# Expert slots that hold a row's id and gate instead of the row, with the rows fetched from the output

## Chip, cores, metric

The kernel runs on one core of one Trainium2 chip. The metric is the device time of that core in microseconds, median of several runs. An engine is one of the core's five instruction streams: TensorE (PE, its weight loads PEld), VectorE (DVE), ScalarE (ACT), GpSimd (POOL) and SyncE (SP), which here issues nearly all DMAs.

## What is computed

First a linear attention with a state for each of 4 batches x 8 heads, 768 steps, 48 channels, then a mixture of 8 experts over the 3,072 rows of 384 numbers (8 heads x 48) that come out of it:

```python
for t in range(S):                                   # B, H, S, D = 4, 8, 768, 48
    state = alpha[:, :, t, :, None] * state + np.einsum('bhd,bhe->bhde', k[:, :, t], v[:, :, t])
    y[:, :, t] = np.einsum('bhd,bhde->bhe', q[:, :, t], state)
x = y.transpose(0, 2, 1, 3).reshape(B * S, H * D)    # 3072 x 384
out = x.copy()
xc = x[x @ w_skip > 0]                               # only these rows see an expert
e_idx = np.argmax(xc @ w_gate, axis=1)               # one of E = 8
gate_w = softmax(xc @ w_gate)[chosen expert]
h = np.maximum(xc[e_idx == e] @ w1[e], 0.0)          # 384 -> F = 1024
out[those rows] = xc + gate_w * (h @ w2[e])          # 1024 -> 384
```

So about half of the rows are left as they are, and each of the others goes through one expert.

## The kernel before

**Attention.** `static_path` runs 24 chunks: chunk i holds the heads of batch i % 4 for 128 steps. The rows of a chunk come out as one tile `x` of 128 rows x 386 numbers: 384 of the row, one for its id (its number in the output) and one for its gate. In chunk order, VectorE does two scans over the decays (`decay`, L233 and L241, written three chunks ahead of their use), GpSimd multiplies them into k and q (L244, L245), TensorE makes the scores (L254), the transposes of k (L268), the products with the state (`inter`), with v (`outer`, `intra`) and the turn back to rows together with the router's products (`rows`, L337); VectorE updates the state (`carry`, L322 and L325). ScalarE copies the rows to `x` (L343), and SyncE stores them in the output (L345): every row is written there, and the rows that pass an expert are written again later. The instructions of an engine run in the order in which the program is written (`manual_schedule`); a tile pool with n buffers makes a writer wait for the readers of n tiles before.

The inputs of a chunk are loaded by SyncE four chunks ahead (`load`, L217 for the first five, L220 and L223): `qka` (decays, q and k; five buffers, two DMAs of 48x1541 for a chunk) and `vt` (128x384). On the same queue go the row stores, the pieces of the experts' weights (`weight_pieces`, L492, 128x768 of `raw`, which has two buffers) and the clears, below.

**Routing.** `route_expert` (groups of three chunks) and `route_one` (the last six chunks singly) find the expert of each row, its gate and whether it is skipped; `route_rank` and `route_slot` make from running counts a slot number: row n of expert e goes to slot e*3072 + n, a skipped row to a number out of bounds, which the DMA drops. `scatter` (L474, GpSimd) writes the 128 rows of `x`, 386 numbers each, into their slots of `xs` in DRAM. An expert has 256 slots that are used (a run with more is done again by a general path, which does not run here). The slots that no row takes must hold something: `clear_pieces` (L141 to L150) writes zeros and an id out of bounds into 256 slots of each expert, eight DMAs of 386 KB, two in each of the first four chunks, from a tile `empty` that GpSimd fills (L146, L147).

**The seam.** The experts use rows of all chunks, but expert 0 starts before the last three chunks (21 to 23, `LATE` = 21 and above) have been scattered: `early_rows` (L435) loads expert 0's 256 slots as they are, with the rows of chunks 0 to 20, and `early_turn` (L449) transposes them on TensorE; the rows of the last three chunks are added by products with a matrix of ones and zeros (`late_rows`, from high and low parts made by `late_split`, L456 and L457, into the same sums). The last three scatters stand behind that in the program.

**Experts.** For each expert `gather` (L530) loads its 256 slots with two DMAs of 128 rows into `xr` (three buffers), two experts ahead; `turn` (L557) transposes them on TensorE, ScalarE and VectorE split them in high and low parts; `up` (L577) makes 18 products of 128x128 by 128x256 for a pair of column blocks, ScalarE (L581) and VectorE (L582) take the relu and split it, `down` (L593) makes 24 products for each half, VectorE (L596) multiplies by the gate `xr[:, j, 385]` and adds the row, and GpSimd scatters 128 rows to the output by their ids (L598). Both products run three times, high by high, low by high and high by low. The weights are split in the same way by ScalarE (`hi`, L508) and by VectorE or GpSimd (`lo`, L512; tiles `w1h`, `w1l`, `w2h`, `w2l`) for the next expert while one runs. During the first experts `guard` loads all alphas (L541, `alpha`, one buffer) and ScalarE looks whether one lies outside a range (L545, `over`).

## Time and profile before

| | |
|---|---|
| time, median of 3 runs | 333.29 us (332.33 to 333.87) |
| profiled execution: its time | 333.48 us |
| its span | 331.8 us |
| mean granted clock of TensorE | 0.917 |
| TensorE busy (products / weight loads) | 292.5 / 270.2 us, 88% / 81% |
| VectorE, ScalarE, GpSimd busy | 226.9, 152.6, 184.3 us (68%, 46%, 56%) |
| DMA | 66.15 MB in 29,420 packets, mean 199 GB/s; 4,466 packets under 512 B |

How to read it: the span goes from the first to the last instruction that the profiler shows; the time of the run is 1.7 us more. The page gives the span in 40 slices with the busy share of each engine in tenths. A row of an engine in order of time reads: start, duration (both us), engine, line, operation, output <- inputs, shapes, how many, and in brackets the idle time of that engine ahead of it with what ended it. SPq is the part of SyncE that issues DMAs; its durations are those of the issuing, not of the transfer. A busy share is a mean over stages in which different engines set the pace, so the stages are looked at one by one.

### The profile page before, as it was taken

How to read it: one execution, taken by the hardware profiler on the slowest of the kernel's cores; microseconds unless marked ns; L12 is line 12 of the kernel's file. 1: busy time of each engine (PE TensorE's matmuls, PEld its weight loads, DVE VectorE, ACT ScalarE, POOL GpSimd, SP SyncE). 2: the span in 40 equal slices, each digit the busy share in tenths (PEclk: the TensorE clock that was granted, in tenths of full speed). 3: DMA queues.
4: the chain of work that ended last, by engine and by line, in shares of the span. 5: the costliest groups of instructions: out<-in, count | busy, mean ns of one | idle time of the engine just before them, and what ended most of it. 6: DMA issues, size and time to landing. Idle time of an engine off the chain costs nothing. (4 is left out here: it accounts for less than half of the span.)

```text
span 331.8 us, 7365 instructions
## 1 busy us (share of the span) xinstructions
PE 292.5 (88%) x2778; PEld 270.2 (81%) x2778; DVE 226.9 (68%) x453; ACT 152.6 (46%) x298; POOL 184.3 (56%) x205
## 2 busy tenths in 40 slices
PE   5877879998699986858898999999999999999991
PEld 5766768887588775646677999999999899999991
DVE  8995578899979999999437664738183555455320
ACT  5122422353435414402424657958595976455200
POOL 6093432589888988866524445444655355464311
PEclk9578785999879999995959999999999999999997
DMA  7949999999976867773546574949688586751000
GB/s 230 281 133 250 252 283 250 223 257 224 236 148 152 183 157 176 197 193 97 155 125 201 166 235 157 398 137 379 215 285 314 193 331 229 242 172 63 12 19 29
DMA packets 29420, 66.15 MB, mean 199 GB/s; under 512 B 4466, under 2 KB 15456, under 8 KB 29376
## 3 DMA queue, kind: packets, MB, share of 16 engines
q1 hardware_dynamic: 26816, 60.76, 63.6%
q0 software_dynamic: 2560, 4.83, 4.2%
q8 instruction: 24, 0.39, 0.5%
q14 instruction: 20, 0.16, 0.2%
HBM read 52.87 MB, written 15.77 MB: 207 GB/s over the span
## 5 line engine op out<-in xcount | busy, mean ns | idle before, releaser
L254 PE MATMUL ps_s<-qka 48*128 48x128 f32 x384 | 31.8, 308 | 23.8 <-POOL qka L244 12.0
L244 POOL TENSOR_TENSOR qka<-qka,sfx 112x512 f32<-112x512 f32 x22 | 27.7, 1257 | 42.4 <-DVE sfx L241 30.7
L254 PEld LDWEIGHTS ps_s<-qka 48*128 48x128 f32 x384 | 26.9, 209 | 29.0 <-POOL qka L244 13.5
L582 DVE SCALAR_TENSOR_TENSOR hl<-ps_h,hh 128x512 fp32r<-128x512 f32 x32 | 22.1, 690 | 33.5 <-ACT hh L581 33.3
L593 PE MATMUL ps_o<-w2h,hh 128*128 128x384 f32 x128 | 43.6, 341 | 0.0
L598 POOL DMA_INDIRECT out_dram<-o,xr x16 | 18.6, 1162 | 45.0 <-DVE o L596 45.0
L593 PE MATMUL ps_o<-w2h,hl 128*128 128x384 f32 x128 | 43.0, 336 | 0.0
L593 PE MATMUL ps_o<-w2l,hh 128*128 128x384 f32 x128 | 43.0, 336 | 0.0
L233 DVE TENSOR_TENSOR_SCAN pfx<-qka,seed 112x516 f32<-112x516 f32 x24 | 34.0, 1418 | 11.0 <-DMA qka<-in_qka_dram 11.0
L343 ACT COPY x<-ps_g 128x384 f32<-128x384 f32 x23 | 11.0, 480 | 65.5 <-DVE logit L338 23.7
L512 POOL TENSOR_TENSOR w2l<-raw,w2h 128x512 fp32r<-128x512 f32 x24 | 31.2, 1302 | 13.5 <-ACT w2h L508 13.1
L474 POOL DMA_INDIRECT xs<-x,slot x24 | 29.9, 1244 | 12.2 <-DVE on L386 4.9
L577 PE MATMUL ps_h<-xh,w1h 128*128 128x256 f32 x192 | 34.2, 284 | 1.2 <-DVE hl L582 1.2
L310 ACT COPY xt<-ps_y 48x512 f32<-48x512 f32 x48 | 27.8, 580 | 13.6 <-PE ps_y L305 12.8
L577 PE MATMUL ps_h<-xh,w1l 128*128 128x256 f32 x192 | 33.8, 282 | 0.0
L241 DVE TENSOR_TENSOR_SCAN sfx<-qka,seedb 112x515 f32<-112x515 f32 x24 | 32.3, 1347 | 1.5
L577 PE MATMUL ps_h<-xl,w1h 128*128 128x256 f32 x192 | 33.3, 282 | 0.0
L305 PE MATMUL ps_y<-st,vt 128*48 128x128 f32 x384 | 32.9, 313 | 0.0
L512 POOL TENSOR_TENSOR w1l<-raw,w1h 128x512 fp32r<-128x512 f32 x16 | 22.3, 1395 | 18.7 <-issue 10.4
L581 ACT ACTIVATE hh<-ps_h 128x512 fp32r<-128x512 f32 x32 | 19.1, 597 | 27.6 <-PE ps_h L577 27.6
L261 DVE COPY_PREDICATED st<-mask,ps_s 128x1024 f32<-128x1024 uint8 x24 | 30.9, 1286 | 0.0
L596 DVE SCALAR_TENSOR_TENSOR o<-ps_o,xr 128x384 f32<-128x384 f32 x16 | 9.9, 616 | 30.3 <-PE ps_o L593 30.3
(141 smaller groups left out, 667.5 us busy)
## 6 DMA issues: line engine op xcount, KB each, us to landing
raw<-in_w_dram SPq DMA_DIRECT2D x64, 384.0 KB
qka<-in_qka_dram SPq DMA_DIRECT2D x38, 288.9 KB
vt<-in_v_dram SPq DMA_DIRECT2D x24, 192.0 KB
out_dram<-x SPq DMA_DIRECT2D x24, 192.0 KB
alpha<-in_nat_dram SPq DMA_DIRECT2D x8, 576.0 KB
xr<-xs SPq DMA_DIRECT2D x18, 193.0 KB
xs<-empty SPq DMA_DIRECT2D x8, 386.0 KB
qka<-in_first_dram SPq DMA_DIRECT2D x3, 674.2 KB
```

What stands on the lines that cost most here:

```text
L233: nc.vector.tensor_tensor_scan(pfx[:PD].rearrange("p a t -> p (a t)"), w["qka"][:PD, 0:n], self.seed1[:PD], 0.0, ALU.mult, ALU.max)
L241: nc.vector.tensor_tensor_scan(sfx[:PD, 0:n - 1][:, ::-1], w["qka"][:PD, 2:AW][:, ::-1], seed[:PD, 2:AW][:, ::-1], 0.0, ALU.mult, ALU.add)
L244: (eng or nc.gpsimd).tensor_tensor(w["kh"][:PD], w["kh"][:PD], after, ALU.mult)
L254: nc.tensor.matmul(ps[:, h, p * P:(p + 1) * P], lhsT=kh[r, p, :], rhs=qh[r, p, :], start=True, stop=True)
L261: self.nc.vector.copy_predicated(w["st"], self.mask, w["ps"])
L305: nc.tensor.matmul(ps[h][64 * h:64 * h + D, p, :], lhsT=v[:, o:o + D], rhs=w["st"][:, h, p * P:(p + 1) * P], start=(i < B and p == 0), sto ...
L310: nc.scalar.copy(out=xt[r], in_=ps[h][r])
L474: ins = nc.gpsimd.indirect_dma_start(out=self.xs[:, :], out_offset=bass.IndirectOffsetOnAxis(ap=self.slot[:, i, :], axis=0), in_=x, in_off ...
L512: eng.tensor_tensor(lo[:, s], raw[:, s], hi[:, s].bitcast(F32), ALU.subtract)
L577: nc.tensor.matmul(ps[:, u, :], lhsT=a[:, k, f * P:(f + 1) * P], rhs=b[:, k, :], start=(n == 0), stop=(n == len(order) - 1))
L582: nc.vector.scalar_tensor_tensor(out=hl, in0=ps, scalar=0.0, in1=hh.bitcast(F32), op0=ALU.max, op1=ALU.subtract)
L593: nc.tensor.matmul(ps, lhsT=a[:, f, js], rhs=b[:, f, :], start=(n == 0), stop=(n == 3 * FT - 1))
```

## The change

A slot of `xs` is now 8 bytes, id and gate; the rows themselves are read back from the output, where `rows` has stored them.

- `empty` is a constant of 128x2x2 numbers, filled at the start by VectorE and GpSimd. One clear of 16 KB for all experts stands in chunk 2 of the loop (L152 in the new numbering), instead of eight in chunks 0 to 3.
- The slots are laid out so that partition p holds slots 2p and 2p+1 (`slots`, and `slots0_i` to match).
- `scatter` (L497) writes 8 bytes a row.
- `early_rows` loads the ids and gates of expert 0 (`meta`, SyncE) and then fetches its rows from the output with two indirect DMAs of GpSimd (`fetch_rows`, L457) into `xr0`. A slot without a row keeps what its buffer held, so `xr0` is zeroed at the start by two ScalarE copies. From this tile `clear_late` also writes zeros into the output rows of chunks 21 to 23 (three DMAs of 192 KB, in chunk 14), which get their own values later. The stores of the rows of chunks 22 and 23 wait for the two early fetches, which read the output.
- `metas` loads the ids and gates of all experts with one DMA behind the last scatter (1,024 pieces of 16 B). `gather` fetches the rows of an expert with two indirect DMAs of GpSimd into one of three buffers that VectorE zeroes once (`xrb`). Those of experts 1 and 0 are issued behind the first quarter of expert 0's `up`; those of expert e + 2 behind `turn(e + 1)` instead of at the start of expert e.
- The gate and the id in `down` come from `meta`, and `xr` has 384 columns.

```diff
-        self.xs = dram.tile([E * N, XW], F32, name="xs")
+        self.xs = dram.tile([E * N, 2], F32, name="xs")
...
-    def clear_pieces(self):
-        nc = self.nc
-        empty = self.const.tile([P, XW], F32, name="empty")
-        nc.gpsimd.memset(empty, 0.0)
-        nc.gpsimd.iota(empty[:, DM:DM + 1].bitcast(I32), pattern=[[0, 1]], base=OFF, channel_multiplier=0)
-        for e in range(E):
-            yield nc.sync.dma_start(out=self.xs[e * N:e * N + CAP, :].rearrange("(j p) w -> p j w", p=P),
-                                    in_=empty.unsqueeze(1).to_broadcast([P, NB, XW]))
+    def slots(self, e0, e1):
+        return self.xs.rearrange("(e n) w -> e n w", e=E)[e0:e1, :CAP, :].rearrange("e (p j) w -> p e (j w)", j=NB)
+
+    def clear(self):
+        nc = self.nc
+        nc.sync.dma_start(out=self.slots(0, E),
+                          in_=self.empty.rearrange("p j w -> p (j w)").unsqueeze(1).to_broadcast([P, E, 2 * NB]))
+
+    def clear_late(self):
+        nc = self.nc
+        for i in range(LATE, NT):
+            row = self.row(i)
+            nc.sync.dma_start(out=self.out[row:row + P, :], in_=self.xr0[:, 0, :])
...
     def early_rows(self):
-        for j in range(NB):
-            ins = nc.sync.dma_start(out=self.xr0[:, j, :], in_=self.xs[j * P:(j + 1) * P, :])
-            self.after(ins.ins, "xs")
-            self.early.append(ins.ins.name)
+        meta = self.late.tile([P, NB, 2], F32, name="meta0")
+        ins = nc.sync.dma_start(out=meta.rearrange("p j w -> p (j w)"), in_=self.slots(0, 1).rearrange("p e w -> p (e w)"))
+        self.after(ins.ins, "xs")
+        self.early = [ins.ins.name]
+        self.fetch_rows(self.xr0, meta)
+
+    def fetch_rows(self, xr, meta):
+        return [self.nc.gpsimd.indirect_dma_start(
+            out=xr[:, j, :], out_offset=None, in_=self.out[:, :],
+            in_offset=bass.IndirectOffsetOnAxis(ap=meta[:, j, 0:1].bitcast(U32), axis=0),
+            bounds_check=N - 1, oob_is_err=False) for j in range(NB)]
...
-            in_=x, in_offset=None, bounds_check=E * N - 1, oob_is_err=False)
+            in_=x[:, DM:DM + 2], in_offset=None, bounds_check=E * N - 1, oob_is_err=False)
...
+        self.xrb = [self.mp.tile([P, NB, DM], F32, name=f"xr{i}", bufs=1) for i in range(3)]
+        for t in self.xrb:
+            self.nc.vector.memset(t, 0.0)
+
+    def metas(self):
+        self.meta = self.mp.tile([P, E, NB, 2], F32, name="meta", bufs=1)
+        ins = self.nc.sync.dma_start(out=self.meta.rearrange("p e j w -> p e (j w)"), in_=self.slots(0, E))
+        self.after(ins.ins, "xs")
 
     def gather(self, e):
-        xr = self.mp.tile([P, NB, XW], F32, name="xr", bufs=3)
-        for j in range(NB):
-            s = e * N + j * P
-            ins = self.nc.sync.dma_start(out=xr[:, j, :], in_=self.xs[s:s + P, :])
-            self.after(ins.ins, "xs")
-        self.ew[e] = dict(xr=xr)
+        xr, meta = self.xrb[e % len(self.xrb)], self.meta[:, e]
+        for ins in self.fetch_rows(xr, meta):
+            self.disjoint(ins.ins, "out")
+        self.ew.setdefault(e, {}).update(xr=xr, meta=meta)
...
                 if i + 4 < NT:
                     self.load(i + 4)
-                advance(clear, 2)
+                if i == 2:
+                    self.clear()
+                if i == 14:
+                    self.clear_late()
...
-            for e in (1, 0):
-                self.gather(e)
+            self.metas()
...
-                if e + 2 < E:
-                    self.gather(e + 2)
                 for g in range(FT // 2):
                     self.up(e, g)
                     advance(split, 2)
+                    if (e, g) == (0, 0):
+                        for n in (1, 0):
+                            self.gather(n)
                 if e + 1 < E:
                     self.turn(e + 1)
+                if e + 2 < E:
+                    self.gather(e + 2)
```

How the order of two engines changes, at the two places of which the prediction speaks. SyncE's queue from the load of chunk 4's `vt` on (`qka` with its buffer's number, `xs<-empty` the clears, `out_dram<-x` the store of a chunk's rows, `raw` a piece of weights), before:

```order
L223 DMA vt<-in_v_dram 128x384
L149 DMA xs<-empty 128x2x386 x2
L220 DMA qka_128<-in_qka_dram 48x1541 x2
L223 DMA vt<-in_v_dram 128x384
L149 DMA xs<-empty 128x2x386 x2
L345 DMA out_dram<-x 128x384
L220 DMA qka_129<-in_qka_dram 48x1541 x2
L223 DMA vt<-in_v_dram 128x384
```

and after:

```order
L240 DMA vt<-in_v_dram 128x384
L237 DMA qka_132<-in_qka_dram 48x1541 x2
L240 DMA vt<-in_v_dram 128x384
L362 DMA out_dram<-x 128x384
L237 DMA qka_133<-in_qka_dram 48x1541 x2
L240 DMA vt<-in_v_dram 128x384
L152 DMA xs<-empty 128x8x4
```

The two pairs of clears that stood ahead of the loads of chunks 5 and 6 are gone, and the one that is left stands behind them; the store of chunk 0's rows keeps its place ahead of the load of chunk 6.

GpSimd where the experts begin (`w1l`, `w2l`: low parts of expert 1's weights; `xr_...<-out_dram` a fetch of 128 rows, of expert 1, of expert 0 and of expert 2 in this order; `out_dram<-o` the scatter of an expert's result), before:

```order
L474 DMA xs<-x,slot 24576x386 x3
L512 TENSOR_TENSOR w1l<-raw,w1h 128x512 x2
L512 TENSOR_TENSOR w2l<-raw,w2h 128x512
L598 DMA out_dram<-o,xr 3072x384
L512 TENSOR_TENSOR w2l<-raw,w2h 128x512
```

and after:

```order
L497 DMA xs<-x,slot 24576x2 x3
L535 TENSOR_TENSOR w1l<-raw,w1h 128x512
L457 DMA xr_2328<-out_dram,meta 128x384 x2
L457 DMA xr_2327<-out_dram,meta 128x384 x2
L535 TENSOR_TENSOR w1l<-raw,w1h 128x512
L535 TENSOR_TENSOR w2l<-raw,w2h 128x512
L457 DMA xr_2329<-out_dram,meta 128x384 x2
L628 DMA out_dram<-o,meta 3072x384
```

Four fetches have come between the two `w1l` pieces, and two more ahead of the first scatter to the output; before, rows came by SyncE's plain loads and none of this stood on GpSimd.

26 lines of the change are left out of this document (16 added, 10 removed).

## Prediction

> **What bounds the kernel now.** I read the page's slices first, then the order of time on VectorE and on SyncE's queue for the first 63 us, then the seam between attention and experts (165 to 205 us), then the chain of waits. The profiled execution took 333.48 us, 331.8 of it span; the median shown is 333.29. My sum is made against the 333.48 and moved to the median by subtracting 0.2.
>
> The slices, 331.8 / 40 = 8.3 us each (PEclk is the clock that TensorE was granted, in tenths):
>
> ```profile
> PE   5877879998699986858898999999999999999991
> ...
> DVE  8995578899979999999437664738183555455320
> ...
> PEclk9578785999879999995959999999999999999997
> DMA  7949999999976867773546574949688586751000
> ```
>
> Three stages. From slice 22 TensorE is at 9 nearly throughout: the expert products set the pace and nothing in the change shortens them. From about 58 to 150 us VectorE is at 9: the attention chunks go at its pace. But in slices 3 to 6 (25 to 58 us) the DMA engines stand at 9, and VectorE at 5 to 8. That stretch in order of time, by the scan that opens each chunk and the state update that closes the one before:
>
> ```profile
> 25.44 0.36 DVE L325 TENSOR_TENSOR state<-ps_v,pfx 112x192 f32<-112x192 f32 x1 [0.66 <-PE ps_v L295]
> 29.05 1.23 DVE L233 TENSOR_TENSOR_SCAN pfx<-qka,seed 112x516 f32<-112x516 f32 x1 [3.25 <-DMA qka<-in_qka_dram]
> ```
> ```profile
> 51.11 1.23 DVE L233 TENSOR_TENSOR_SCAN pfx<-qka,seed 112x516 f32<-112x516 f32 x1 [2.04 <-DMA qka<-in_qka_dram]
> ...
> 56.55 1.22 DVE L233 TENSOR_TENSOR_SCAN pfx<-qka,seed 112x516 f32<-112x516 f32 x1
> ...
> 62.27 1.27 DVE L233 TENSOR_TENSOR_SCAN pfx<-qka,seed 112x516 f32<-112x516 f32 x1
> ```
>
> The view of that scan's line over 20 to 63 us sums its idle time:
>
> ```profile
>   DMA qka<-in_qka_dram: 10.7, 4
> ```
>
> Four waits for the loads of qka (the scans of chunks 5 to 8), 10.7 us. The reason stands in SyncE's queue in order of time, in the list of its waits (total, times, longest) and in the sizes of its transfers:
>
> ```profile
> 20.44 2.37 SPq L149 DMA_DIRECT2D xs<-empty  x2
> 22.92 0.95 SPq L220 DMA_DIRECT2D qka<-in_qka_dram  x2
> ...
> 25.45 0.58 SPq L345 DMA_DIRECT2D out_dram<-x  x1
> 26.12 2.32 SPq L220 DMA_DIRECT2D qka<-in_qka_dram  x2
> ```
> ```profile
> SPq L149 <- POOL empty L147: 8.6, 1, 8.6
> ```
> ```profile
> xs<-empty SPq DMA_DIRECT2D x8, 386.0 KB
> ```
>
> The first clear waits 8.6 us, to 20.44, for its fill, which GpSimd writes only behind a chunk's products, and every load behind it on the queue waits along. Then eight clears, 8 x 386 KB = 3.16 MB, go out among the loads. Two stretches of equal length (busy time of the engines, then granted clock, DMA share, GB/s):
>
> ```profile
> 20.00:63.00 43.00, 37.73 (x421) 33.15 (x423) 30.12 (x55) 12.27 (x24) 20.26 (x27) 0.76 0.96 248
> 63.00:106.00 43.00, 38.71 (x528) 33.40 (x526) 40.18 (x80) 17.92 (x37) 36.32 (x42) 0.92 0.86 205
> ```
>
> At 248 GB/s the clears hold the DMA engines for 12.7 us, a little more than VectorE waits.
>
> **The change part by part. A, the clears.** They become one transfer of 16 KB, behind the loads of chunk 6, with its fill ready in the first microseconds. In SyncE's rows, in the section on the change, the loads of chunks 5 and 6 no longer stand behind anything that waits for GpSimd. The load of chunk 5 (22.92 now) goes as soon as chunk 0's buffer is free, at the latest where the queue now begins to wait, 20.44 - 8.6 = 11.8, so 11 us earlier; its scan then starts where the state update ends, 25.44 + 0.36 = 25.8, not 29.05. The load of chunk 6 still stands behind the row store at 25.45, so it leaves at about 26 as now, but with no clears before it. From there chunks follow at the rate of the two unblocked ones above, 56.55 - 51.11 = 5.4 and 62.27 - 56.55 = 5.7 us, the first two, with less routing, near 5.0. So the scan now at 62.27 starts near 25.8 + 5.0 + 5.0 + 5.7 + 5.7 + 5.7 = 52.9, a gain of 9.4. What is late next: TensorE, whose clock is 0.76 in this stretch against 0.92 after, and the loads, because a chunk's loads, store and weight piece are 1.38 MB (2 of 48x1541, 2 of 128x384 and one of 128x768 numbers of 4 bytes), 5.6 us at 248 GB/s, about the chunk's period. I take 8.0. Bounds: 10.7 (all the waits) and 4.5, if every chunk from 5 to 9 takes 0.5 us longer for loads and the first two 1.2 more for a slow TensorE (9.4 - 2.5 - 2.4).
>
> **B, the start.** VectorE gets one memset of four columns, ScalarE two copies of 128x384. A copy of 128x448 and the idle time ahead of it:
>
> ```profile
> 11.06 0.53 ACT L270 COPY kt<-ps_k 128x448 f32<-128x448 f32 x1 [4.43 <-PE ps_k L268]
> ```
>
> Two copies of at most 0.53 vanish in 4.43. The memset is the one addition on the path, between 0 and the same 0.53; for four columns I take 0.1. **C, the three late clears** of the output, 3 x 192 KB at chunk 14, stand ahead of chunk 19's load: 0.59 MB at 205 GB/s is 2.9 us of DMA time at a place where the engines are 0.86 busy. Taken at 0.2, bounds 0 and 2.9.
>
> **D, the early rows of expert 0.** Before, two plain loads of 128 rows. Now a load of ids, then two fetches by GpSimd that need the ids, with `late_split`'s subtractions queued behind them.
>
> GpSimd's rows at the seam in order of time:
>
> ```profile
> 177.34 1.01 POOL L457 TENSOR_TENSOR latel<-x,lateh 128x384 fp32r<-128x384 f32 x1 [4.73 <-ACT lateh L456]
> ```
> ```profile
> 183.11 0.97 POOL L474 DMA_INDIRECT xs<-x,slot  x1 [0.30 <-issue]
> ```
> ```profile
> 188.67 1.54 POOL L512 TENSOR_TENSOR w1l<-raw,w1h 128x512 fp32r<-128x512 f32 x1 [0.17 <-ACT w1h L508]
> ```
>
> The view of the tile of fetched rows, TensorE's and SyncE's (count, duration in ns min/median/max, first and last start), then that of the output scatter, the nearest thing to a fetch:
>
> ```profile
> L449 PE MATMUL ps_s<-ident,xr x8: 273/275/356, 177.7 to 180.4; 128*128 128x128 f32 x8
> L557 PE MATMUL ps_x<-ident,xr x6: 272/272/273, 191.0 to 191.6; 128*128 128x128 f32 x6
> ```
> ```profile
> L530 SPq DMA_DIRECT2D xr<-xs x6: 326/430/432, 185.8 to 188.1; - x6
> L435 SPq DMA_DIRECT2D xr<-xs x2: 327/376/425, 173.1 to 173.5; - x2
> ```
> ```profile
> L598 POOL DMA_INDIRECT out_dram<-o,xr x16: 968/1188/1192, 197.0 to 325.8; - x16
> ```
> ```profile
> DMA to landing us min/median/max: 2.4/2.7/4.6
> ```
>
> No row has a fetch by id, or a small load. A scatter to the output, 128 rows too, takes 1.19 us of GpSimd and lands 2.4 to 4.6 us after its start, 2.7 in the middle. Ids asked for at 173.1 land at 175.5 to 177.7; the fetches start there and 1.19 later and land at 177.9 and 179.1 in the good case, 182.3 and 183.5 in the bad one, against a first use from 177.7 and a last at 180.4. So +0.2 to +3.1 (183.5 - 180.4); the subtraction at 177.34 starts at most 0.6 late in the good case, as GpSimd idled 4.73 ahead of it. Against that, rows of 8 bytes may land sooner than rows of 1,544. I take +0.5.
>
> The Trainium skill speaks against the small pieces: "DMA: Bandwidth & Descriptors", in Specifications, asks for at least 512 B a piece for line rate and says that less is written as read-modify-write. No run here shows a piece of 16 B; by the fit on that page (about 2.0 us and the bytes) the load of ids would take 2.0 us, an estimate, and the sum would stay within half a microsecond of mine.
>
> **E, the rows of expert 1.** All ids are loaded by one transfer at 185.8 (like the loads now, it waits for the last scatter, 183.11, to land). In 1,024 pieces of 16 B it lands at 188.2 to 190.4, I take 189.4. Then GpSimd fetches: second half started 1.19 later, 190.6, landed at 193.3 with 2.7, against the second half of the transposes, now at 191.4. TensorE waits 1.9 (0.4 with 2.4 everywhere, 4.8 with 4.6 everywhere).
>
> **F, the four fetches ahead of other work on GpSimd.** Its rows in the section on the change show it: the second `w1l` moved behind four fetches and their wait for the ids: 189.4 + 4 x 1.19 = 194.2 instead of 188.67. It frees the buffer that the loads at 191.68 wait for, so these leave near 195.7, 4 us late, and with them the alpha pieces behind them on the queue, for which ScalarE stands still ahead of expert 1's first activation. SyncE's queue, ScalarE in order of time, and a piece of the chain of waits:
>
> ```profile
> 191.68 2.13 SPq L492 DMA_DIRECT2D raw<-in_w_dram  x4
> ```
> ```profile
> 201.04 1.26 ACT L545 ACTIVATE over<-alpha,lim 128x1152 bf16<-128x1152 f32 x1 [5.33 <-DMA alpha<-in_nat_dram]
> ```
> ```profile
> 203.68 0.58 ACT L581 ACTIVATE hh<-ps_h 128x512 fp32r<-128x512 f32 x1
> ```
> ```profile
> 252.15 4.73 DMA alpha<-in_nat_dram
> ```
>
> The activation at 203.68 would come near 207.7. TensorE runs on in its other product buffers, so most is covered, but the chain of waits at 252.15 still runs through that loop of ScalarE and loads, which is then 4 us late where E has already made TensorE 1.9 late. Of the difference, 2.1, I count 1.3, since the rows no longer go through SyncE's queue; bounds 0 and 2.5. Later fetches (two per expert, 2.4 us) lie in GpSimd's idle time ahead of the output scatter and have a whole expert to land; without that cover each expert's weights would come 2.4 later.
>
> ```profile
> 214.59 1.19 POOL L598 DMA_INDIRECT out_dram<-o,xr  x1 [3.24 <-DVE o L596]
> ```
>
> **Sum:** -8.0 + 0.1 + 0.2 + 0.5 + 1.9 + 1.3 = -4.0: 329.5 for an execution like the profiled one, **329.3** beside the median.
>
> **Rivals.** *The seam costs more than the start gives (slower).* One mechanism: ids, then rows, two landings in series, with GpSimd held between. With the ends of the rows D is 3.1, E 4.8 and F 2.5, with C at its 2.9 and A at 8: +5.4, 338.7 beside the median; halfway between these and my values it is +0.7, 334.0. It decides once a load of ids and a fetch take some 4.3 us each to land. For it: landings of 4.6 occur. Against it: the median beside the experts is 2.7. The clock would add to it: slice 1 has 5 tenths, and the same group of products takes 1.92 us at one time and 1.05 at another:
>
> ```profile
> 28.82 1.05 PE L337 MATMUL ps_g<-xw,xt 112*128 112x105 f32 x8
> ```
> ```profile
> 34.87 1.92 PE L337 MATMUL ps_g<-xw,xt 112*128 112x105 f32 x8
> ```
>
> Half a slice, 4.1 us, at the low rate after a long wait at E would cost 4.1 x (1 - 1.05/1.92) = 1.9 more. The Trainium skill has this as a rule, in "TensorE: Matmul & The Clock Gate", Part 1: a window of about 3.4 us without work brings the clock to half; slice 1 agrees, and by that window the price would be 1.7. Chance 0.10.
>
> *The early wait only changes its name.* TensorE at its low clock, or loads at a chunk's period, hold the first chunks; A is 4.5 and the rest stands: -0.5, 332.8. For it: 1.38 MB a chunk is 5.6 us. Against it: chunks at 51.11 and 56.55 ran through with the same weight pieces on the queue. Chance 0.17. That the change does not do what it says belongs here too: the row store at 25.45 still gates chunk 6.
>
> *The seam is free.* Fetches land at 2.4, ids too, loads are lighter without the rows on SyncE: A is 9, D and F a few tenths, E 0.4: -8, 325.3. Chance 0.15.
>
> **How the numbers follow.** The forecast, -1.7 to -6.5 us, 326.8 to 331.6, has 0.58. Half a per cent (1.7 us) is about what a measurement here can tell from no change. Faster by more: 0.58 + 0.15 and a part of the second rival, 0.76; same 0.14; slower 0.10. The range, 324.6 to 333.6, leaves out most of the slower rival and the far end of the free seam.
>
> **What would show it.** Right: no DMA wait, or under 3 us in all, ahead of VectorE's scans; the eleventh scan (62.27 now) at 53 to 56; TensorE waiting 0.4 to 4.8 us for expert 1's rows; first activation of expert 1 later against TensorE than now. Wrong: the eleventh scan after 58; or the distance from expert 0's first use of fetched rows (177.7 now) to the end of the span, 154.1 us, longer by over 8 us, or not longer at all.

## The result, and the profile after

The changed kernel is slower: 343.22 us median (342.75 to 345.45), against 332.81 for the kernel before on the same chip; ratio 1.0327, 95% interval 1.0268 to 1.0387. The forecast was 329.3. Its profiled execution has a span of 341.8 us, 10.0 more than before's.

First the slices of the page, then VectorE's scans in order of time, the idle time of their line over 20 to 63 us, and 10-us stretches (columns as before: PE, PEld, DVE, ACT, POOL busy, clock, DMA share, GB/s):

```profile
PE   6869869997997799889839699999989899999991
...
DVE  8997495999999999998435623819265456555310
...
PEclk9658967996999969757978989999999999999998
DMA  8949898898669868942815174959769495741000
```
```profile
41.44 1.23 DVE L250 TENSOR_TENSOR_SCAN pfx<-qka,seed 112x516 f32<-112x516 f32 x1 [4.70 <-DMA qka<-in_qka_dram]
...
60.84 1.23 DVE L250 TENSOR_TENSOR_SCAN pfx<-qka,seed 112x516 f32<-112x516 f32 x1
```
```profile
  DMA qka<-in_qka_dram: 5.2, 2
```
```profile
20.00:30.00 10.00, 9.56 (x82) 8.70 (x83) 9.08 (x12) 2.17 (x4) 6.14 (x7) 0.55 0.37 90
30.00:40.00 10.00, 9.86 (x144) 8.68 (x143) 5.60 (x9) 4.24 (x8) 4.38 (x6) 1.00 1.00 115
40.00:50.00 10.00, 5.94 (x70) 5.22 (x70) 8.49 (x20) 2.82 (x6) 3.95 (x6) 0.80 0.95 257
```

The waits for loads fell from 10.7 to 5.2 us, but one of 4.70 stands at the eighth scan, behind a stretch in which the DMA engines are fully busy and move only 115 GB/s. The eleventh scan comes at 60.84, not at 53 to 56, and the last at 152.17 against 152.41: the start gave nothing. (Seven more kernels below have the same clear; there the last scan starts at 151.45 to 155.99, so no gain hides in the spread.)

The seam. GpSimd's last scatter and its fetches, SyncE's queue, SyncE's waits (total, times, longest) and TensorE at expert 1's turn:

```profile
183.82 0.97 POOL L497 DMA_INDIRECT xs<-x,slot  x1 [0.30 <-issue]
190.30 1.30 POOL L535 TENSOR_TENSOR w1l<-raw,w1h 128x512 fp32r<-128x512 f32 x1 [5.51 <-ACT w1h L531]
192.84 1.05 POOL L457 DMA_INDIRECT xr<-out_dram,meta  x1 [1.23 <-DVE w1l L535]
194.19 1.01 POOL L457 DMA_INDIRECT xr<-out_dram,meta  x1 [0.31 <-issue]
...
197.84 1.29 POOL L535 TENSOR_TENSOR w1l<-raw,w1h 128x512 fp32r<-128x512 f32 x1
```
```profile
180.45 0.82 SPq L362 DMA_DIRECT2D out_dram<-x  x2
181.32 0.94 SPq L515 DMA_DIRECT2D raw<-in_w_dram  x2
189.06 0.38 SPq L555 DMA_DIRECT2D meta<-xs  x1
199.16 1.75 SPq L515 DMA_DIRECT2D raw<-in_w_dram  x4
```
```profile
SPq L362 <- DMA xr<-out_dram,meta: 7.8, 1, 7.8
```
```profile
195.98 0.77 PE L587 MATMUL ps_x<-ident,xr 128*128 128x128 f32 x3 [3.26 <-DMA xr<-out_dram,meta]
197.19 0.90 PE L587 MATMUL ps_x<-ident,xr 128*128 128x128 f32 x3 [0.44 <-DMA xr<-out_dram,meta]
```

And the chain of waits, a few of its longest pieces in order of time:

```profile
183.82 4.98 DMA xs<-x,slot
...
189.06 2.97 DMA meta<-xs
...
200.95 7.63 DMA alpha<-in_nat_dram
...
222.36 5.14 DMA alpha<-in_nat_dram
...
241.31 5.77 DMA alpha<-in_nat_dram
...
260.70 5.28 DMA alpha<-in_nat_dram
```

The last scatter takes 4.98 us to land, then the ids 2.97; the fetches wait for them and the second `w1l` for the fetches, 197.84 instead of 188.67. From there to 266 the chain runs through loads of alpha, ScalarE's looks at them and loads of weights. To see where the 10.0 us lie, I read from the order of time the last scan, the first product of expert 0 (U0), and, counted from U0, the first products of experts 1 and 7 and the end of the span:

| us | eleventh scan | last scan | U0 | expert 1 | expert 7 | end |
|---|---|---|---|---|---|---|
| before | 62.27 | 152.41 | 182.31 | 17.72 | 125.45 | 149.49 |
| after | 60.84 | 152.17 | 183.83 | 23.27 | 133.16 | 157.97 |

To the last scan -0.24, from there to U0 +1.76 (31.66 against 29.90), then +5.55 up to expert 1, +2.16 from there to expert 7 (109.89 against 107.73) and +0.77 at the end: 10.0. (Executions of one kernel fall into faster and slower ones; the ratios compare the faster ones alone, and no stages are read from four kernels further down whose profiled execution was one of the slower.) These are differences of two single traces; how far they vary is said where it matters.

### The profile page after: what moved, and what is told of

Its sections match the earlier page's. It is cut to its first block, busy times and chain, and to the rows that moved or that the text cites. A ratio compares the mean times of both kernels' runs of the same rounds, so it can differ in the third digit from the quotient of the medians.

```text
span 341.8 us, 7389 instructions
## 1 busy us (share of the span) xinstructions
PE 298.9 (87%) x2778; PEld 276.1 (81%) x2778; DVE 230.1 (67%) x457; ACT 153.3 (45%) x300; POOL 201.3 (59%) x222
## 2 busy tenths in 40 slices
DMA packets 27692, 60.33 MB, mean 177 GB/s; under 512 B 6944, under 2 KB 13646, under 8 KB 27648
## 5 line engine op out<-in xcount | busy, mean ns | idle before, releaser
L261 POOL TENSOR_TENSOR qka<-qka,sfx 112x512 f32<-112x512 f32 x22 | 26.8, 1218 | 44.5 <-DVE sfx L258 30.0
L271 PE MATMUL ps_s<-qka 48*128 48x128 f32 x384 | 33.1, 320 | 19.8 <-POOL qka L261 12.1
L271 PEld LDWEIGHTS ps_s<-qka 48*128 48x128 f32 x384 | 28.3, 221 | 25.8 <-POOL qka L261 13.9
L497 POOL DMA_INDIRECT xs<-x,slot x24 | 31.1, 1298 | 10.4 <-POOL x L496 4.9
L258 DVE TENSOR_TENSOR_SCAN sfx<-qka,seedb 112x515 f32<-112x515 f32 x24 | 35.7, 1487 | 1.5
L360 ACT COPY x<-ps_g 128x384 f32<-128x384 f32 x23 | 11.0, 479 | 56.8 <-POOL qka L261 19.4
L628 POOL DMA_INDIRECT out_dram<-o,meta x16 | 18.3, 1146 | 30.3 <-DVE o L626 29.4
L250 DVE TENSOR_TENSOR_SCAN pfx<-qka,seed 112x516 f32<-112x516 f32 x24 | 31.8, 1327 | 6.0 <-DMA qka<-in_qka_dram 5.9
L626 DVE SCALAR_TENSOR_TENSOR o<-ps_o,meta,xr 128x384 f32<-128x384 f32 x16 | 9.9, 618 | 34.5 <-PE ps_o L623 34.3
L354 PE MATMUL ps_g<-xw,xt 112*128 112x105 f32 x184 | 31.2, 322 | 0.0
```

Source lines behind the costliest of these rows:

```text
L250: nc.vector.tensor_tensor_scan(pfx[:PD].rearrange("p a t -> p (a t)"), w["qka"][:PD, 0:n], self.seed1[:PD], 0.0, ALU.mult, ALU.max)
L258: nc.vector.tensor_tensor_scan(sfx[:PD, 0:n - 1][:, ::-1], w["qka"][:PD, 2:AW][:, ::-1], seed[:PD, 2:AW][:, ::-1], 0.0, ALU.mult, ALU.add)
L261: (eng or nc.gpsimd).tensor_tensor(w["kh"][:PD], w["kh"][:PD], after, ALU.mult)
L271: nc.tensor.matmul(ps[:, h, p * P:(p + 1) * P], lhsT=kh[r, p, :], rhs=qh[r, p, :], start=True, stop=True)
L354: nc.tensor.matmul(pg[:, p, :], lhsT=w["xt"][:PD, p, :], rhs=self.xw[:PD, p, :], start=True, stop=True)
L497: ins = nc.gpsimd.indirect_dma_start(out=self.xs[:, :], out_offset=bass.IndirectOffsetOnAxis(ap=self.slot[:, i, :], axis=0), in_=x[:, DM:D ...
```

## Experiments

Times on different chips differ by a per cent, so ratios to the kernel before on the same chip are given, and the stages are read from each kernel's own profile. The theory after the comparison: the small clear, not its bytes but its pieces, ate the start; at the seam two chains are late, the rows of expert 1 and the loop in which weight loads, alpha loads and ScalarE wait for one another. Where that loop is late, TensorE waits for `hl`, the low part of an expert's activations, which VectorE writes behind ScalarE.

**The clear in 8 pieces of 2 KB.**

```diff
-        self.empty = const.tile([P, NB, 2], F32, name="empty")
+        self.empty = const.tile([E, CAP, 2], F32, name="empty")
...
-        nc.sync.dma_start(out=self.slots(0, E),
-                          in_=self.empty.rearrange("p j w -> p (j w)").unsqueeze(1).to_broadcast([P, E, 2 * NB]))
+        nc.sync.dma_start(out=self.xs.rearrange("(e n) w -> e (n w)", e=E)[:, :CAP * 2],
+                          in_=self.empty.rearrange("p j w -> p (j w)"))
```

> The one clear writes the same 16 KB in 8 pieces of 2 KB instead of 1,024 pieces of 16 B; nothing else changes. Theory (small pieces): in the changed kernel the DMA engines were fully busy from 30 to 40 us at only 115 GB/s, and VectorE's eighth scan waited 4.7 us for its load, because the 1,024 pieces of the clear sit in all DMA queues ahead of it; then that wait goes to under 1 us, the eighth scan starts near 37 instead of 41.4, TensorE does not drop its clock behind it, and the eleventh scan starts at 54 to 56 instead of 60.8. If that lead lasts to the end of the attention, the time falls by 4 to 6 us, to 337 to 339. Rival (the loads themselves are the limit: a chunk moves 1.2 to 1.4 MB): the wait moves to another chunk, the eleventh scan stays above 59 and the time within 1 us of 343.2.

Ratio 1.0168 (1.0065 to 1.0271). Its scans, the same stretch, and the idle time of the scans' line over 20 to 63 us:

```profile
38.93 1.42 DVE L250 TENSOR_TENSOR_SCAN pfx<-qka,seed 112x516 f32<-112x516 f32 x1 [0.59 <-DMA qka<-in_qka_dram]
...
56.30 1.22 DVE L250 TENSOR_TENSOR_SCAN pfx<-qka,seed 112x516 f32<-112x516 f32 x1
```
```profile
30.00:40.00 10.00, 8.90 (x134) 7.85 (x132) 7.78 (x11) 4.49 (x9) 4.79 (x6) 1.00 0.96 218
```
```profile
  DMA qka<-in_qka_dram: 2.4, 3
```

The same 16 KB in 8 pieces: 218 GB/s instead of 115 in that stretch, a wait of 0.59 instead of 4.70, the waits of that line 2.4 us in all, the last scan at 147.03 instead of 152.17. The lead lasts to the end of the attention. The page counts 1,024 DMA packets fewer (26,668 instead of 27,692) for the same 60.33 MB. In the packets of the two traces, the 1,024 pieces all start between 31.1 and 32.5 us; from 33 to 38 a row of qka (6,164 B) then takes 1.08 us on average, against 0.40 with 8 pieces. So the time is lost less in the pieces themselves than in the transfers behind them; by what means, no run tells. The other traces agree: 0.9 to 1.5 us with pieces of 16 B, 0.4 to 0.5 with pieces of 2 KB. With the tile filled by ScalarE instead of GpSimd (with GpSimd's fill the fifth scan had come at 22.14 instead of 20.50; that the fill did it is not shown, as it lies anywhere from 20.3 to 21.6 in the kernels that left the fill alone):

> The changed kernel with the clear in 8 pieces of 2 KB, as run before, but its tile filled by ScalarE instead of by GpSimd, which had made the fifth scan 1.6 us later (22.1 instead of 20.5). It shows what the start is worth without that: the fifth scan at 20.3 to 20.8, the eleventh at 54 to 55.5 instead of 56.3, the last at 145 to 146.5 instead of 147.0, the time 1 us under the run with GpSimd's fill, ratio 1.010 to 1.016. Rival (the start is held by the loads, not by that fill): the eleventh scan stays at 56 and the ratio at 1.017.

Fifth scan 20.98, eleventh 55.47, last 146.36; ratio 1.0169 (1.0088 to 1.0251). The scans are near what was expected, but the 0.7 us at the last one don't show in the time: the ratio is the rival's. In a third kernel with this clear and this fill, further down (the last of three with later alphas), the fifth scan came at 23.07, the eleventh at 58.44 and the last at 149.16, so the gain of the mended clear varies, 3.3 to 6.1 us in these three.

**Order at the seam, one thing at a time.** The four fetches behind both `w1l` pieces (`(e, g) == (0, 1)` instead of `(0, 0)`):

> The four fetches of experts 1 and 0 stand behind both w1l pieces on GpSimd (after the second quarter of expert 0's first products) instead of between them. Theory (two chains at the seam, and the later one is the loop of weights, alpha loads and ScalarE): the second w1l starts at 191.5 to 192.5 instead of 197.84, the four weight loads and the alpha load behind it leave about 6 us earlier (193 to 194 instead of 199.2), the waits of TensorE for hl in experts 3 to 5 (2.9 us in all) go to under 1; expert 1's rows come at most 0.5 later. Time 2 to 3 us lower, 340 to 341.5. Rival (rows alone: TensorE's wait at expert 1's turn is all that counts): no change, 342.7 to 343.7.

Wrong on both counts: ratio 1.0464 (1.0377 to 1.0552), above the changed kernel's 1.0327, though the intervals just meet. The second `w1l` did start at 192.77 and the weight loads left at 195.54, but TensorE waited longer for the rows:

```profile
194.46 1.33 POOL L457 DMA_INDIRECT xr<-out_dram,meta  x1
196.10 1.46 POOL L457 DMA_INDIRECT xr<-out_dram,meta  x1 [0.31 <-issue]
```
```profile
195.54 1.75 SPq L515 DMA_DIRECT2D raw<-in_w_dram  x4
```
```profile
199.16 0.90 PE L587 MATMUL ps_x<-ident,xr 128*128 128x128 f32 x3 [5.03 <-DMA xr<-out_dram,meta]
202.94 0.90 PE L587 MATMUL ps_x<-ident,xr 128*128 128x128 f32 x3 [2.88 <-DMA xr<-out_dram,meta]
```

Two fetches that landed in 3.1 and 3.0 us (192.84 to 195.98, 194.19 to 197.19) now take 4.7 and 6.8: the weight loads let go earlier seem to share the DMA engines with them. The turn of expert 1 behind the first half of `down(0)`:

```diff
-                if e + 1 < E:
+                if 0 < e and e + 1 < E:
                     self.turn(e + 1)
...
                 for j in range(NB):
+                    if e == 0 and j == 1:
+                        self.turn(1)
                     self.down(e, j)
```

> For expert 1 alone the turn of its rows stands behind the first half of expert 0's second products instead of ahead of both, so that TensorE has 4.2 us of work while the rows are fetched. Theory (two chains): TensorE's wait for expert 1's rows (3.7 us) goes to under 1, its clock does not drop there, expert 1's first products start at 201.5 to 203.5 instead of 207.1; but the loop of weights, alpha loads and ScalarE is as late as before, so TensorE waits for hl instead, 5 to 8 us instead of 2.9, and the time falls by only 0 to 1.5 us. Rival (rows alone): the 5 us stay won, 338 to 339.

Ratio 1.0344 (1.0227 to 1.0461), no gain. TensorE's waits in the experts:

```profile
PE ps_h L607 <- DVE hl L612: 5.7, 3, 4.1
PE ps_x L587 <- DMA xr<-out_dram,meta: 0.6, 1, 0.6
```

Expert 1 starts at U0 + 18.59 instead of 23.27, and all of it is lost within that expert (expert 2 at 42.84, 40.92 in the changed kernel): the wait has only moved. The last weight pieces ahead of the row stores (`advance(fetch, 3 if i == NT - 1 else 1)`):

> The last two weight pieces of expert 1 are issued ahead of the load of expert 0's ids and of the row stores that wait for the two early fetches (7.8 us on SyncE's queue), so at about 168 instead of 181.3. Theory: they land before 175, ScalarE's and GpSimd's first w1 pieces start about 3 us earlier (187 instead of 190.3); the last scatter, which then shares the DMA engines with no weight piece, lands in 2.4 to 3.5 us instead of 5.0, if it was the sharing that made it slow, so that ids, rows and the weight loop come 1.5 to 5 us earlier: 338 to 341.5. Rival (8-byte writes land slowly by themselves): the last scatter still takes 4.5 us or more to land, the four fetches still wait for the ids, and the time falls by less than 1.5 us; if the early pieces slow down the ids of expert 0, TensorE's wait ahead of expert 0 (5.4 us) grows and eats that too.

Ratio 1.0381 (1.0291 to 1.0472), no gain: the load of the ids left 3.83 us after the last scatter's start (186.50 to 190.33) instead of 5.24, but the early rows had become later (from the last scan to U0 33.79 us instead of 31.66). VectorE alone makes expert 1's `w1l`:

```diff
-                eng = nc.gpsimd if n % 5 in (1, 3) else nc.vector
+                eng = nc.gpsimd if n % 5 in (1, 3) and (e, name) != (1, "w1") else nc.vector
```

> In the changed kernel the low parts of expert 1's w1 are made by VectorE alone, so that neither w1l stands on GpSimd around the four fetches; nothing else moves. Theory now, after the run in which the fetches were moved behind both w1l pieces and rows landed in 5 to 7 us instead of 3 (the weight loads that are let go earlier share the DMA engines with the fetched rows): the weight loads leave at 192 to 193 instead of 199.2, the first two fetches start at 192.0 instead of 192.8 but land in 4 to 6 us, expert 1's turn is as late or 1 to 3 us later, and the stretch from the last scan of VectorE to the end is 188 to 191 us, against 189.6: no gain. Rival (order alone, the loop of weights and alpha loads sets the end): rows land in 3 us as before, the stretch falls to 184 to 187 and the time by 3 to 5 us.

Ratio 1.0462 (1.0393 to 1.053): weight loads at 194.26, the first fetch, started 1.8 us ahead of them, lands in 3.1 us (192.44 to 195.49), the second in 5.8 (193.79 to 199.60), expert 1 at U0 + 26.90. Contention again, and it costs more than expected: expert 1 is 3.6 us later, not 1 to 3, and the stretch from the last scan to the end is 193.5 us, not 188 to 191.

**Why the last scatter lands late.** In the kernel before, only the scatters are changed: 8 bytes into the first columns of the old slots of 1,544, and then 8 bytes into an array of its own with slots of 8 (`xp2`; the diff is this second one's). Both leave the rows out, so only their order in time is read, in one run each.

```diff
-            out=self.xs[:, :], out_offset=bass.IndirectOffsetOnAxis(ap=self.slot[:, i, :], axis=0),
-            in_=x, in_offset=None, bounds_check=E * N - 1, oob_is_err=False)
+            out=self.xp2[:, :], out_offset=bass.IndirectOffsetOnAxis(ap=self.slot[:, i, :], axis=0),
+            in_=x[:, DM:DM + 2], in_offset=None, bounds_check=E * N - 1, oob_is_err=False)
```

> The kernel before, with its 386-number slots, clears and loads, but each scatter writes only the id and the gate (8 bytes a row) into its slot; the rows themselves are left out, so the experts work on zeros. The order of all engines and all other transfers is as before. Theory (8-byte writes are slow to land by themselves): the scatters near 161 to 162 us and the last one, which landed 2.4 us after their start before, land after 4 to 8 us, and the loads of the slots behind the last scatter start near 188 instead of 185.8. Rival (it was the weight pieces that the changed kernel issued later, 181.3 instead of 178.2, that shared the DMA engines with the last scatter): the landing stays at 2.4 to 3 and the loads start near 185.8.

> The kernel before, but each scatter writes its 8 bytes a row into a separate array with slots of 8 bytes side by side, as in the changed kernel, while the loads of the experts read the old slots, which hold only what the clears wrote: rows and ids are left out, so no row comes from an expert. Loads, clears and weight pieces are those of before, and the loads of slots still wait for the scatters. In the runs so far the first load behind the last scatter left 2.4 to 2.7 us after that scatter's start in three kernels with slots of 1,544 bytes, 3.8 us in two kernels with slots of 8 bytes and no weight piece issued in the 4 us ahead, 4.8 to 6.0 where a weight piece was issued 2 to 3 us ahead. Theory (small writes to neighbouring places take longer to land): 3.4 to 4.0 us here. Rival (only the transfers beside it count): 2.4 to 2.8 us.

The last scatter and the first load that waits for it, with wide slots and then with narrow ones:

```profile
183.95 0.97 POOL L475 DMA_INDIRECT xs<-x,slot  x1 [0.30 <-issue]
```
```profile
186.32 2.70 SPq L531 DMA_DIRECT2D xr<-xs  x6
```
```profile
184.30 0.97 POOL L475 DMA_INDIRECT xp<-x,slot  x1 [0.30 <-issue]
```
```profile
187.72 2.70 SPq L531 DMA_DIRECT2D xr<-xs  x6
```

2.37 us with wide slots, so 8-byte writes by themselves are not slow; 3.42 with narrow ones, at the lower edge of what neighbouring writes should cost. The rest of the changed kernel's 5.24 goes with the weight pieces: 3.7 to 3.8 in the three changed kernels without one in the 4 us ahead, 4.3 to 6.1 in the eight with one. Only one of the three was made to test this (the weight pieces ahead of the row stores, 3.83); in the other two it came about.

**Both chains together, and the alphas.** The clear in 2-KB pieces filled by GpSimd, `w1l` on VectorE, and the turn of expert 1 behind both halves of `down(0)`:

> The changed kernel with three repairs: the clear in 8 pieces of 2 KB, expert 1's w1l on VectorE alone, and expert 1's turn behind both halves of expert 0's second products, so that the fetched rows have 8 us more. Theory (two chains at the seam, both repaired here): the last scan starts at 147 to 148, the weight loads leave 6 us earlier, TensorE waits under 2 us for rows and under 4 for hl, the stretch from the last scan to the end is 183 to 187 instead of 190, and the time lies within 2 us of the kernel before, ratio 0.99 to 1.005. Rival (the chain from the last scatter over ids to rows cannot be covered by moving work of TensorE): the stretch stays at 189 or more, ratio 1.01 to 1.02.

Ratio 1.0069 (1.0025 to 1.0113): the best of the changed kernels, between the two expectations and still behind the kernel before. Then the alpha loads one expert later, alone, with the turn moved, and with the turn and the clear:

```diff
-                if e == 0:
-                    check = self.guard()
+                if e < 2:
+                    check = self.guard() if e else iter(())
```

> The changed kernel with the eight alpha loads and ScalarE's looks at them begun one expert later (two per expert in experts 1 to 5 instead of 0 to 4; the test of their result moves from expert 5 to 6). So ScalarE does not stand still for alpha ahead of expert 1's activations. Theory (two chains, equally late): expert 1's rows still come 5 us late, the waits of TensorE for rows stay at 3 to 4 us, those for hl after expert 1 (2.9 us) go under 1; the stretch from the last scan to the end is 186.5 to 188.5 instead of 189.6, the time 1 to 3 us lower than the changed kernel's. Rival (the loop alone sets the end): 183 to 185. Rival (rows alone): 189 to 190.

> The last one, and expert 1's turn behind the first half of expert 0's second products, so that its rows have 4.2 us more. With the turn alone the stretch was 190.7 us, TensorE's wait for rows 0.6 and for hl 5.7. Theory (two chains, equally late): both waits are under 1.5 now and the stretch is 183 to 186. Rival (the loop of weights itself, by the second w1l behind four fetches, sets the end without the alphas too): TensorE still waits over 3 us for hl and the stretch stays over 187.

> The last one with the clear in 8 pieces of 2 KB, its tile filled by ScalarE. If start and seam are mended independently, the last scan starts at 146 to 147 and the stretch behind it is 183 to 186: a span of 329 to 333, ratio to the kernel before 0.985 to 1.0. If the seam is not mended, 336 to 338 and a ratio over 1.01.

Ratios 1.0425 (1.0275 to 1.0576), 1.0346 (1.0216 to 1.0476) and 1.0207 (1.0116 to 1.0297): no gain, and my theory that mending both gives 183 to 186 us from the last scan to the end fell (188.4 in the second, 188.0 in the third). With the turn moved, the waits in the experts were

```profile
PE ps_h L607 <- DVE hl L612: 5.1, 4, 1.8
PE ps_o L623 <- DVE hl L612: 0.3, 1, 0.3
```

Experts 1 and 2 ran nearly as in the kernel before (U0 + 17.84 and 36.00; before 17.72 and 35.35), and the loss came back as waits for `hl` in experts 2 to 5. The loop is not late at one place: while alphas are in it, a round seems to take longer than an expert. The chain of waits of the changed kernel has the alpha loads at 222.36, 241.31 and 260.70, 19.0 and 19.4 us apart; TensorE needs 17.6 to 17.7 for an expert. So the alphas were taken out altogether, their loads and ScalarE's looks at them (`check = iter(())`; that check of the inputs is left out), in three kernels, one run each.

> The changed kernel without the alpha loads and ScalarE's looks at them (that check of the inputs is left out). Counted from the start of expert 0's first products, because what lies before varies. Theory (the loop with alphas takes 19 us a round, TensorE 17.6; a late loop binds until the alphas are over): expert 1's first products still start near 23.3 us, for the rows; from there to those of expert 7 it is 6 x 17.65 = 106 us instead of 109.9, no wait for hl is left, and the end lies at 153.5 to 154.5 instead of 158.0. Rival (the waits for hl come from the weights alone, by the second w1l behind the fetches): expert 7's still start over 109 us after expert 1's, the end at 157 or later.

> The changed kernel with expert 1's turn behind the first half of expert 0's second products, and without the alpha loads and ScalarE's looks at them (left out). Theory (rows, and the loop by its alphas): both are gone, expert 1's first products start at 17.8 to 18.8 us, expert 7's at 124 to 125.5, the end at 148.5 to 150.5, as in the kernel before (149.5). Rival (the weights alone): a wait for hl of over 3 us stays in expert 1 or 2 and the end is at 152 or later.

> The kernel before without the alpha loads and ScalarE's looks at them (left out), as the control. Theory: the two waits for hl (1.2 us) go with what the clock loses behind them, expert 7's first products start at 17.7 + 6 x 17.65 = 123.6 us, the end at 147.5 to 148. Rival: waits for hl stay, the end at 149 or later.

| us from U0 | expert 1 | expert 7 | end | waits for rows / hl in the experts |
|---|---|---|---|---|
| changed | 23.27 | 133.16 | 157.97 | 3.7 / 2.9 |
| changed, no alphas | 23.61 | 130.09 | 154.86 | 3.8 / none |
| changed, turn moved | 18.59 | 133.77 | 158.64 | 0.6 / 5.7 |
| changed, turn moved, no alphas | 18.16 | 125.35 | 150.25 | 0.2 / 0.4 |
| before | 17.72 | 125.45 | 149.49 | none / 1.2 |
| before, no alphas | 17.72 | 123.80 | 148.19 | none / none |

The waits without alphas, in the changed kernel and with the turn moved:

```profile
PE ps_x L587 <- DMA xr<-out_dram,meta: 3.8, 2, 3.1
```
```profile
PE ps_o L623 <- DVE hl L612: 0.4, 1, 0.4
PE ps_x L587 <- DMA xr<-out_dram,meta: 0.2, 1, 0.2
```

All is near what the theory had; two of the ends lie 0.2 and 0.4 us above its figures.

Only without the alphas is anything won by moving the turn, 4.6 us (154.86 to 150.25), where with them it was lost again. This tells the shares apart, roughly: the loop with alphas costs 3.1 us in the changed kernel (157.97 - 154.86) and 1.3 before (149.49 - 148.19), so 1.8 of the 8.5 come from it, 4.6 from the rows, and 2.1 (150.25 - 148.19) remain, about 0.4 of it before expert 1, 1.1 up to expert 7 and 0.5 behind. Where those come from was not tried. In other traces with the loop as it was the end lies at U0 + 148.0 to 151.5 with the old seam and at 159.0 and 159.3 with the new one (the two with only the clear mended), so each share can be off by 1 to 2 us. Nor do the runs tell the alphas' bytes from ScalarE's looks at them.

Counting from U0 also leaves something out. The three took 342.66, 339.66 and 329.25 us; the second is 10.4 behind the third, of which only 2.1 lie behind U0. Its last scan is 3.1 later (155.99 against 152.88), and from there to U0 it takes 31.76 us against 26.53.

**The kernel before with a mend of its own.** The tile of its clears filled early, the clears where they were; then, with the fill by ScalarE, one clear a chunk instead of two; and the early fill with the alphas one expert later:

```diff
+        self.empty = const.tile([P, XW], F32, name="empty")
+        nc.gpsimd.memset(self.empty, 0.0)
+        nc.gpsimd.iota(self.empty[:, DM:DM + 1].bitcast(I32), pattern=[[0, 1]], base=OFF, channel_multiplier=0)
         self.lim = const.tile([P, 2], F32, name="lim")
```

> The kernel before with one thing moved: GpSimd fills the tile of the clears among its first constants, so that the first clear does not wait for it; the eight clears of 386 KB stay where they are. This parts the two halves of what I had counted for the start. If it was the stuck queue (8.6 us): the load of chunk 5 leaves at 12 to 13 instead of 22.9, the waits of VectorE for loads fall from 10.7 us to 3 to 6, the eleventh scan starts at 56 to 59 instead of 62.3, and the time falls by 3 to 5 us. If it was the 3.16 MB of the clears: the queue is free earlier but the same bytes stand ahead of the same loads, the waits stay over 8 us, and the time is within 1.5 us of before.

> The kernel before with the fill of the clears' tile made early by ScalarE, as the last version did by GpSimd, and with one clear of 386 KB in each of the first eight chunks instead of two in each of the first four. Theory (after the stuck queue, the bytes of two clears ahead of each chunk's loads are what VectorE still waits for, 8.0 us): spread out, each chunk has 386 KB less ahead of its loads up to chunk 8, the waits fall to 4 to 6 us and the time by another 1 to 3 us, ratio 0.985 to 0.992. Rival (the same 3.16 MB have to pass before the first scatter at about 60 us, and the weight pieces come on top from chunk 3 on): the waits only move to later chunks, ratio 0.99 to 0.998.

> The kernel before with the early fill of the clears' tile by GpSimd (as run before, ratio 0.993) and the alpha loads one expert later. The loop's waits in the kernel before are 1.2 to 2.5 us of TensorE for hl. If the alphas make them, the stretch from the last scan to the end falls from 177.6 to 175 to 176.5 and the ratio to 0.983 to 0.99. If not, 0.99 to 0.995.

The first: ratio 0.9927 (0.9876 to 0.9978), the only version here whose interval lies below the kernel before, by 0.7%. The waits fell from 10.7 to 7.8 us, the eleventh scan to 60.03, the last to 151.10. With 2.4 us of waits left where the bytes are gone too (the clear in 8 pieces), the stuck queue was the smaller part, 2.9, and the bytes the larger. The second: 0.9978 (0.993 to 1.0026), the third: 0.9964 (0.9897 to 1.0031). Both have the early fill too and neither is better, so that gain is small and not sure.

## Why the prediction was wrong

**A, -8.0, measured -0.24 at the last scan: the step that failed first.** The working counted the new clear as "one transfer of 16 KB" and so at nothing. It is 1,024 pieces of 16 bytes, and SyncE's queue issued it at 28.35, ahead of the loads of chunk 7. Up to there the lead was being won (the scan of chunk 6 at 32.40 instead of 36.02); the wait at chunk 7's took over half of it. With 8 pieces the start gives 5.4 us (152.41 - 147.03), 6.1 (146.36) and, in a third kernel, 3.3 (149.16), against bounds of 4.5 and 10.7, so the reading of the stuck queue and the clears was sound and their size too large. The Trainium skill, "DMA: Bandwidth & Descriptors", section Specifications, says that below 512 B the DMA does read-modify-write and asks for 512 B for line rate; on the rate this case's trace agrees (115 GB/s against 218), the read-modify-write itself no run shows. I had cited that rule for the load of the ids, where it hardly mattered (2.97 us; I had 3.6), and not for the clear, where it did. Nor did I work out that citation rightly: ids landing in 2.0 us would have lowered E alone by 1.6, so my sum would not have stayed within half a microsecond.

**B and C** can't be parted here. From the eleventh scan to the last the kernel with the mended clear takes 90.73 us, against 90.14 before. But four other kernels with the old clears take 90.8 to 91.5 there, so C can't be told from nothing.

**D, +0.5, measured 1.76** from the last scan to U0 in this pair, inside its bounds. But the kernel before had a long stretch in its profile: it was 26.5 to 29.9 us in five kernels with the old seam and 30.3 to 33.8 in eleven with the new one, 27.4 and 31.9 in the middle. So D is more likely about 4 us, above its bound of 3.1, and one more term that was much too small. The ids were asked for at 172.15, the first fetch started at 175.97 and landed at 179.04: 3.1 us for the fetch, and 3.8 from the ids to it, between the 2.4 and the 4.6 of my two cases. TensorE waited 5.4 us for that fetch, and behind the wait its granted clock was 0.50 from 179.0 to 182.4; the same four transposes before and after:

```profile
177.71 0.61 PE L449 MATMUL ps_s<-ident,xr 128*128 128x128 f32 x4
```
```profile
179.04 1.22 PE L472 MATMUL ps_s<-ident,xr 128*128 128x128 f32 x4 [5.38 <-DMA xr<-out_dram,meta]
```

Of the eleven, eight wait there for fetched rows, 1.7 to 5.7 us; the other three don't and are as long, with a mean granted clock of 0.63 to 0.65 over the stretch. How these two go together was not tried.

**E, +1.9, measured 5.55, outside its upper bound of 4.8.** The mechanism was right and the start of the sum wrong. I let the ids be asked for "at 185.8 (like the loads now, it waits for the last scatter, 183.11, to land)", taking the 2.7 us of before for granted. They left at 189.06, or, counted from U0, 5.23 us behind it instead of 3.49. The stores of the last chunks' rows wait on SyncE's queue for the early fetches (7.8 us), and the weight pieces behind them leave at 181.32 instead of 178.18 and run beside the last scatter, whose 8-byte writes lie side by side besides. From there the ids took 2.97 us (I had 3.6), GpSimd started the first fetch 0.8 later, and the fetches took 3.1 and 3.0 (I had 2.7). The products behind TensorE's wait then ran slower, the first five at 0.52 to 0.67 us instead of 0.34, at a granted clock of 0.50:

```profile
197.74 0.67 PE L623 MATMUL ps_o<-w2h,hh 128*128 128x384 f32 x1
198.21 0.52 PE L623 MATMUL ps_o<-w2l,hh 128*128 128x384 f32 x1
...
199.71 0.34 PE L623 MATMUL ps_o<-w2h,hh 128*128 128x384 f32 x1
```

The Trainium skill's "TensorE: Matmul & The Clock Gate", Part 1, gives half the clock after about 3.4 us without work; the clock of 0.50 agrees, though the waits here were 3.26 and 0.44 us, the longer one a little short of that.

**F, +1.3, measured about 1.8** by the runs without alphas, with an uncertainty of 1 to 2 us. The order was read rightly (second `w1l` behind four fetches, 197.84; I had 194.2 from an earlier start of the ids), and so was the loop. What I lacked was that a round of it, 19.0 to 19.4 us, is longer than an expert, so that a lost lead isn't covered by TensorE's other buffers but paid until the alphas are through. That the late `w1l` and not something else made the loop late is argued: both runs that moved nothing but it or the fetches also let the weight loads collide with the fetches.

Of the rivals, the one with the seam as the loser was right about the place and the mechanism (two landings in series, GpSimd held between) and wrong about the point from which it decides: a load of ids and a fetch took 3.0 us each, not 4.3; most of the time was lost in the landing ahead of them. The rival by which the early wait only changes its name came closest at the start, but named the loads' own bytes and TensorE's clock for it, not the new clear, and priced it at 4.5 us of gain left; nothing was left. Two signs of being wrong that the prediction named came: the eleventh scan after 58, and 162.8 us instead of 154.1 from the first use of fetched rows to the end, 8.7 longer.

## What to carry to other kernels

Count a transfer by its pieces as well as its bytes: with a clear of 16 KB in 16-byte pieces VectorE's waits were 5.2 us in all, with the same bytes in 2-KB pieces 2.4, and with the 3.16 MB that they replaced, and its late fill, 10.7. Where a load becomes ids and then rows, begin the sum where the ids' own writers land, and look up in the new order what runs beside them: a store that now waits on a queue moves all transfers behind it into that place. Find a loop's slack before calling it covered: here one round of it took 19 us against 17.6 of the engine that it feeds, and taking it out of both kernels told in three runs what the reorderings hadn't. And look how far a stage varies between traces of the same code before a pair of them is taken for its price: the stretch ahead of U0 looked like 1.76 us and is more likely about 4.

## What the runs showed of the hardware

- 1,024 pieces of 16 B to DRAM: DMA engines at a share of 1.00 and 115 GB/s over 10 us, and a wait of 4.70 us for the load behind them; with 8 pieces of 2 KB, 218 GB/s and 0.59. The pieces all start within 1.4 us; rows of 6,164 B in the 5 us behind them take 1.08 us on average instead of 0.40.
- Scatters of up to 128 rows of 8 B (skipped rows have a slot out of bounds) landed, to the next load, in 2.37 us with slots 1,544 B apart and in 3.42 with slots 8 B apart, one run each.
- A fetch of up to 128 rows of 1,536 B by ids landed in 3.0 to 3.5 us without weight loads beside it, and in 4.7 to 6.8 with four loads of 384 KB of which the first was issued within 1.1 us of its start.
- Behind a wait of TensorE of 5.38 us its granted clock was 0.50 for 3.4 us, and four products that had taken 0.61 us took 1.22.
